# Ranks of the gate's tiles: one behind each of three second-layer matmul groups, in PSUM columns of their own

## The chip, the cores and the metric

The kernel runs on one core of one Trainium2 chip. The metric is the device time of one execution in microseconds, as the median of the runs shown. One more execution was recorded by the hardware profiler; its rows are what the text reads. TensorE is called PE in the rows, VectorE DVE, ScalarE ACT, GpSimd POOL and SyncE SP.

## What is computed

Three layers in a row: an attention, a dense feed-forward layer of 2304 tokens with 2048 hidden units, and a layer of 8 experts of which each token takes the one with the largest gate logit. Cut to what matters:

```python
# attention: a local band (|i - j| < 4) plus attention on means of 4 rows; 4 batches x 8 heads x 576 x 64
x = np.ascontiguousarray(attn_out.transpose(0, 2, 1, 3)).reshape(B * S, H * D)   # 2304 x 512
h = x @ w_in                                                                     # 512 -> 2048
sp = np.where(h > 20.0, h, np.log1p(np.exp(np.minimum(h, 20.0))))
x = (h * np.tanh(sp)) @ w_out                                                    # 2048 -> 512
...
logits = x @ w_gate + modality_bias[modality_id]                                 # 8 experts
e_idx = np.argmax(logits, axis=1)
...
for e in range(E):
    mask = e_idx == e
    h = np.maximum(x[mask] @ w1[e], 0.0)                                         # 512 -> 1024
    out[mask] = gate_w[mask, None] * (h @ w2[e])                                 # 1024 -> 512
```

## The kernel before

The 2304 tokens of the dense layer are cut into five blocks (512, 512, 512, 384 and 384 tokens, numbered 0 to 4), a block into tiles of 128 tokens (four or three). The 2048 hidden units are 16 chunks of 128, worked in steps of four chunks (`GF = 4`), so a block has four steps, `gi` 0 to 3. A step of `moe1` does two loops over its four chunks. In the first, `layer1` makes a chunk's hidden values in one of the PSUM banks bk0 to bk3 (line 698, 12 matmuls per chunk) and `act1` begins the activation. In the second, `mish` ends the activation (ScalarE's sine, then VectorE's line 718, which reads the bank) and `finish` splits the product in two parts (line 727), while `layer2` runs one step behind: it multiplies a chunk of the step before with the second weights and adds to the banks from bk4 on, one bank for each tile. One call of `layer2` is called a second-layer group here: line 738, three matmuls of 512 columns for each tile, so 12 in a block of 512 tokens and 9 in one of 384.

When a block is done, its tiles are gated while the next block runs. `gates` hands out, a few at a time, the 8 dots of each tile (line 621, VectorE, 512 wide); behind the eighth, `gate_l` finds the tile's experts (lines 632 to 642) and the tile goes to the list `done`. Last comes the rank, `gate_r`: each token's place among the tokens of its expert, over all tiles so far. PE multiplies the tile's one-hot rows with a triangle (line 652) and adds the running count `run` of all tiles before (line 653), in 8 columns of a PSUM bank (columns 16 to 23 of bk0; of bk7 in the last block). VectorE reads them (line 656), makes the place (lines 657 to 659) and adds the tile to `run` (line 660). POOL scatters the token numbers to that place in DRAM (line 661), and SP stores the tile's logits (line 651). Ranks have to be made in the order of the tiles, since each one needs the count that the one before left.

The order on every engine is the order in which the code is written; nothing reorders it. In the second loop of a step all tiles in `done` are ranked behind the second group (`n == 1`). With the pace of `gates`, the first tile of a block is done in step 1, two tiles in step 2, and the fourth, where there is one, in step 3. So in step 2 of each of the blocks 1 to 4 two ranks stand directly behind each other. These are called a pair below, and the blocks are named after the block that runs at that time. The last three tiles of all are ranked later, in the expert layer (`rest`). In block 4, `ahead_2` also stands in this loop: it splits the weight pieces of the first experts, VectorE converting one (line 963) and POOL subtracting (line 964). `fixed_slot` (its count is line 664) then picks the experts to begin with.

Of the kernel before, what the change touches and what calls it, by code (L numbers as in the profile page):

```python
# [15 lines left out]
ALU = mybir.AluOpType  # L16
# [7 lines left out]
def moe_kernel(ctx: ExitStack, tc: tile.TileContext, q, k, v, w_in, w_out, modality, w_gate, w_gate_t, m_bias, w1, w2, out):  # L24
    nc = tc.nc
    V, A, G, PE, SP = nc.vector, nc.scalar, nc.gpsimd, nc.tensor, nc.sync
# [4 lines left out]
    E = w_gate.shape[1]  # L31
# [27 lines left out]
    def table(name, shape, dt=F32):  # L59
        return cp.tile(shape, dt, name=name)  # L60
# [6 lines left out]
    ebase = table("ebase", [128, E])  # L67
# [6 lines left out]
    tri = table("tri", [128, 128], BF16)  # L74
    one_b = table("one_b", [128, 128], BF16)
# [6 lines left out]
    bk = [psp.tile([128, 512], F32, name=f"bk{i}") for i in range(8)]  # L82
    gps = bk[7]
# [141 lines left out]
    def prep_step(n=1):  # L225
        for _ in range(n):
            if "wo" in wpool or steps[0] < 4 * (2 * GF + 4):
                next(pg, None)
                steps[0] += 1

    def prep_to(n):
        while ticks[0] < min(n, len(order) + LAG):
            next(pg)
            steps[0] += 1
# [369 lines left out]
    rank = cp.tile([128, E], F32, name="rank")  # L604
    run = cp.tile([128, E], BF16, name="run")
# [10 lines left out]
    def gate_v(tl, es):  # L616

        if 0 in es:
            gate[tl] = cp.tile([128, E], F32, tag="g_ll", name="g_ll")
        for e in es:  # L620
            V.scalar_tensor_tensor(wgb["junk"], x2[tl], 1.0, wgb[e], op0=ALU.mult, op1=ALU.mult, accum_out=gate[tl][:, e:e + 1])  # L621
# [7 lines left out]
    def gate_l(tl):  # L629
        lg = cp.tile([128, E], F32, tag="g_lg", name="g_lg", bufs=3)  # L630
        SP.dma_start(out=x2d[128 * tl:128 * tl + 128, :DM], in_=x2.pop(tl))
        V.tensor_tensor(lg, gate.pop(tl), bias[:, tl], op=ALU.add)
        mx = cp.tile([128, 8], F32, tag="g_mx", name="g_mx")
        ix = cp.tile([128, 8], U32, tag="g_ix", name="g_ix")
        ixf = cp.tile([128, 1], F32, tag="g_if", name="g_if")
        oh = cp.tile([128, E], F32, tag="g_oh", name="g_oh", bufs=3)
        ohb = cp.tile([128, E], BF16, tag="g_ob", name="g_ob", bufs=3)
        V.max(mx, lg)
        V.max_index(ix, mx, lg)
        V.tensor_copy(ixf, ix[:, 0:1])  # L640
        V.tensor_scalar(oh, iota_e, ixf, None, op0=ALU.is_equal)
        V.tensor_copy(ohb, oh)
        gate[tl] = (lg, oh, ohb)
# [2 lines left out]
        gate_p(tl)  # L646
        gate_l(tl)

    def gate_r(tl, gps=gps):
        lg, oh, ohb = gate.pop(tl)  # L650
        SP.dma_start(out=x2d[128 * tl:128 * tl + 128, DM:], in_=lg)
        PE.matmul(gps[:, 16:16 + E], tri, ohb, start=True, stop=False)
        PE.matmul(gps[:, 16:16 + E], one_b, run, start=False, stop=True)
        pf = cp.tile([128, 1], F32, tag="g_pf", name="g_pf")
        pi = cp.tile([128, 1], I32, tag="g_pi", name="g_pi", bufs=2)
        V.tensor_tensor(rank, gps[:, 16:16 + E], ebase, op=ALU.add)
        V.tensor_tensor(rank, rank, oh, op=ALU.mult)
        V.tensor_reduce(pf, rank, axis=X, op=ALU.add)
        V.tensor_copy(pi, pf)
        V.tensor_tensor(run, run, ohb, op=ALU.add)  # L660
        G.indirect_dma_start(out=ids_d, out_offset=bass.IndirectOffsetOnAxis(ap=pi, axis=0), in_=tok_id[:, tl:tl + 1], in_offset=None, bounds_check=E * NT - 1, oob_is_err=True)  # L661
# [8 lines left out]
    def tiles(j):  # L670
        return range(T0[j] // 128, (T0[j] + BLK[j]) // 128)

    def load_x(j, kk, t):

        xf[j, kk] = t[:, :BLK[j]]
        SP.dma_start(out=xf[j, kk], in_=xT[128 * kk:128 * kk + 128, T0[j]:T0[j] + BLK[j]])
# [12 lines left out]
    def layer1(j, f):  # L689
        if j == 0:  # L690
            prep_chunk(f)
        wh, wl = wi[f // QF]
        h = bk[f % GF][:, :BLK[j]]
        n = 0
        for kk in range(KD):
            x = pool["x"][:, :, kk, :BLK[j]]
            for a, c in ((wh, 0), (wh, 1), (wl, 0)):
                PE.matmul(h, a[:, f % QF, kk], x[:, c], start=n == 0, stop=n == 3 * KD - 1)  # L698
                n += 1

    def act1(j, f):
        t = pool["t"].tile([128, BT], F32, tag="t", name="t")[:, :BLK[j]]
        if f % GF == 0:
            d = pool["t"].tile([1, 1], F32, tag="d", name="d", bufs=2)
            A.activation(d, half[:1], AF.Sigmoid)
        A.activation(t, bk[f % GF][:, :BLK[j]], AF.Tanh, scale=0.5)  # L706
        A.activation(t, t, AF.Arctan, scale=-0.5, bias=half)  # L707
        th[j, f] = t

    def mish(j, f):  # L710
        t = th.pop((j, f))
        A.activation(t, t, AF.Sin, scale=-2.0, bias=hpi)  # L712
        if late:
            j_, f_, t_, _ = late[-1]
            gg = gt[j_, f_] = pool["b"].tile([128, 2, BT], F32R, tag="gg", name="gg", bufs=GB)[:, :, :BLK[j_]]
            A.copy(gg[:, 0], t_)  # L716
            late[-1] = (j_, f_, t_, gg)
        V.tensor_tensor(t, bk[f % GF][:, :BLK[j]], t, op=ALU.mult)  # L718
        late.append((j, f, t, None))

    def finish():

        j, f, t, gg = late.pop(0)
        if gg is None:
            gg = gt[j, f] = pool["b"].tile([128, 2, BT], F32R, tag="gg", name="gg", bufs=GB)[:, :, :BLK[j]]
            A.copy(gg[:, 0], t)  # L726
        V.tensor_tensor(gg[:, 1], t, gg[:, 0], op=ALU.subtract)  # L727
# [21 lines left out]
    def moe1(bcx, wop):  # L749
        pool["b"] = bcx.enter_context(tc.tile_pool(name="b_wk", bufs=4))  # L750
        for n in range(GF):
            mish(0, n)
            if n:
                finish()

        todo, done = [], []
        for s in range(GF, NB * NF, GF):
            j, f = divmod(s, NF)
            gi = f // GF
            last = gi == NF // GF - 1  # L760
            more = j + 1 < NB
            dec = s <= NF

            def gates(n):
                for _ in range(n):
                    if todo:
                        tl, e = todo.pop(0)
                        gate_v(tl, [e])
                        if e == E - 1:
                            gate_l(tl)  # L770
                            done.append(tl)

            if gi == 1 and j:
                todo += [(tl, e) for tl in tiles(j - 1) for e in range(E)]
            for n in range(GF):
                layer1(j, f + n)
                prep_step(TK1[2 * n])
                if n == 0 and late:
                    finish()
                act1(j, f + n)  # L780
                prep_step(TK1[2 * n + 1])
                if s == NF and n == 2:
                    prep_to(len(order) + LAG)
                    constants_a()
                if not more:
                    ahead_1(gi, n)
                if gi:
                    gates(3)
            if last and j == 0:
                xs = [stp.tile([128, 2, BT], F32, tag="st", name="xs") for _ in range(2)]  # L790
                for kk in range(KD):
                    load_x(1, kk, xs[kk // 2][:, kk % 2])
            for n in range(GF):
                mish(j, f + n)
                prep_step(TK2[2 * n])
                if n:
                    finish()
                layer2(s - GF + n)
                if last and more:
                    split_x(j + 1, n)  # L800
                prep_step(TK2[2 * n + 1])
                if s == NF and n == 2:
                    constants_b(bk[0])
                if n == 1:
                    while done:
                        gate_r(done.pop(0), bk[0] if more else gps)
                if gi:
                    gates(2 if n == 0 else 1)
                if j and more and (gi, n) in ((1, 3), (2, 3)):
                    for kk in range(2 * gi - 2, 2 * gi):  # L810
                        load_x(j + 1, kk, mtp.tile([128, BT], F32, tag="m", name="xs"))
                if not more:
                    ahead_2(gi, n)
        finish()
        for n in range(GF):
            layer2(NB * NF - GF + n)
            ahead_2(NF // GF, n)
# [382 lines left out]
```

## Time and profile before

| | |
|---|---|
| median of 3 runs | 857.98 us (856.6 to 859.43) |
| the profiled execution | 856.72 us, its span 855.0 us |
| PE busy | 777.9 us (91%) |
| VectorE busy | 608.5 us (71%) |
| ScalarE busy | 538.7 us (63%) |
| POOL busy | 224.5 us (26%) |
| mean granted clock of TensorE | 0.955 of full speed |

The span goes from the first to the last instruction of the profiled execution. Busy shares are means over stages that differ: the attention, the dense layer (about 200 to 590 us) and the experts behind it. PE is the engine that the dense layer waits for most of the time, so its list of waits is the view to begin with.

### The profile page before, as it was taken

The numbers are of one execution on the slowest core, as the hardware profiler recorded it, in microseconds if no ns is written. First come the engines' busy times: TensorE is split into PE (matmuls) and PEld (weight loads), VectorE is DVE, ScalarE is ACT, GpSimd is POOL, SyncE is SP. The second block draws the span as 40 slices with busy tenths as digits, with TensorE's granted clock in tenths as the row PEclk, the third lists the DMA queues.
The fourth block names the chain that finished last, engine by engine and source line by source line (L and its number), as shares of the span: only waits on it lengthen the run. The fifth ranks groups of instructions, "written<-read, shape, count | busy, mean of one in ns | idle before, by whom it ended". The sixth has DMA issues, their size and how long they took to land. (4 is left out here: it accounts for less than half of the span.)

```text
span 855.0 us, 14553 instructions
## 1 busy us (share of the span) xinstructions
PE 777.9 (91%) x5110; PEld 654.9 (77%) x5110; DVE 608.5 (71%) x1442; ACT 538.7 (63%) x1003; POOL 224.5 (26%) x212
## 2 busy tenths in 40 slices
PE   6799986799979999999999799979888999999992
PEld 5577664578858878887889689878787889999982
DVE  6799998789975874288248846979776666656652
ACT  4889997798856556655655566644435555555651
POOL 7678764000000000000000001236533123333330
PEclk9789999889989999999999999989989999999997
DMA  8988983546514110011001105425737777777662
GB/s 175 219 197 227 209 213 124 178 143 192 175 49 165 51 38 0 13 45 33 0 1 56 33 0 210 68 12 167 163 124 231 225 247 225 236 225 222 205 204 83
DMA packets 90641, 115.08 MB, mean 135 GB/s; under 512 B 39467, under 2 KB 61629, under 8 KB 90301
## 3 DMA queue, kind: packets, MB, share of 16 engines
q1 hardware_dynamic: 85997, 103.45, 43.9%
q0 software_dynamic: 4560, 10.60, 3.6%
q8 instruction: 42, 0.69, 0.4%
q14 instruction: 42, 0.34, 0.2%
HBM read 98.11 MB, written 16.17 MB: 134 GB/s over the span
## 5 line engine op out<-in xcount | busy, mean ns | idle before, releaser
L718 DVE TENSOR_TENSOR t<-bk,t 128x512 f32<-128x512 f32 (+1 forms) x80 | 50.2, 633 | 94.1 <-ACT t L712 94.1
L661 POOL DMA_INDIRECT ids_by_expert<-tok_id,g_pi x18 | 19.7, 1096 | 288.0 <-DVE run L660 113.2
L621 DVE SCALAR_TENSOR_TENSOR junk<-o,wgb 128x512 f32<-128x512 f32 x120 | 85.0, 708 | 3.0
L706 ACT ACTIVATE t<-bk 128x512 f32<-128x512 f32 (+1 forms) x80 | 44.1, 551 | 59.3 <-PE bk L698 57.4
L727 DVE TENSOR_TENSOR gg<-t,gg 128x512 fp32r<-128x512 f32 (+1 forms) x80 | 54.8, 685 | 14.1 <-ACT gg L726 7.6
L716 ACT CAST gg<-t 128x512 fp32r<-128x512 f32 (+1 forms) x60 | 34.5, 575 | 47.1 <-DVE t L718 28.8
L698 PE MATMUL bk<-x,wi0h 128*128 128x512 f32 (+1 forms) x160 | 51.1, 398 | 6.3 <-DVE x L686 5.1
L707 ACT ACTIVATE t<-t,half 128x512 f32<-128x512 f32 (+1 forms) x80 | 54.6, 682 | 2.6
L1086 POOL DMA_INDIRECT out_dram<-yo,oid x19 | 25.4, 1336 | 111.4 <-ACT yo L1085 65.1
L698 PE MATMUL bk<-x,wi1h 128*128 128x512 f32 (+1 forms) x160 | 48.2, 384 | 5.9 <-DVE t L718 5.9
L712 ACT ACTIVATE t<-t,hpi 128x512 f32<-128x512 f32 (+1 forms) x80 | 52.3, 674 | 0.2
L1072 ACT ACTIVATE hT<-bk 128x256 fp32r<-128x256 f32 x80 | 30.3, 383 | 33.5 <-PE bk L1070 30.6
L738 PE MATMUL bk<-wo1h,gg 128*128 128x512 f32 x144 | 49.5, 417 | 0.0
L1073 DVE SCALAR_TENSOR_TENSOR hT<-bk,hT 128x256 fp32r<-128x256 f32 x80 | 32.9, 420 | 23.2 <-ACT hT L1072 23.2
L698 PE MATMUL bk<-x,wi3h 128*128 128x512 f32 (+1 forms) x160 | 46.2, 370 | 0.0
L698 PE MATMUL bk<-x,wi2h 128*128 128x512 f32 (+1 forms) x160 | 46.1, 369 | 0.0
L738 PE MATMUL bk<-wo3h,gg 128*128 128x512 f32 x144 | 46.1, 392 | 0.0
L738 PE MATMUL bk<-wo0h,gg 128*128 128x512 f32 x144 | 45.9, 392 | 0.0
L738 PE MATMUL bk<-wo2h,gg 128*128 128x512 f32 x144 | 45.8, 392 | 0.0
L698 PEld LDWEIGHTS bk<-x,wi0h 128*128 128x128 f32 x160 | 31.3, 199 | 14.5 <-DVE x L686 7.0
L698 PEld LDWEIGHTS bk<-x,wi1h 128*128 128x128 f32 x160 | 30.9, 196 | 10.8 <-DVE t L718 6.4
L386 ACT COPY spare<-bk 64x512 f32<-64x512 f32 x32 | 35.3, 1104 | 5.7 <-PE bk L375 5.5
(309 smaller groups left out, 2393.1 us busy)
## 6 DMA issues: line engine op xcount, KB each, us to landing
est<-in_moe_w_dram SPq DMA_DIRECT2D x88, 512.0 KB
wst<-in_moe_w_in_dram SPq DMA_DIRECT2D x16, 512.0 KB
wst<-in_moe_w_out_dram SPq DMA_DIRECT2D x16, 512.0 KB
vw<-in_v_dram SPq DMA_DIRECT2D x88, 64.0 KB
v<-in_v_dram SPq DMA_DIRECT2D x16, 288.0 KB
x_t<-x SPq DMA_DIRECT2D x16, 288.0 KB
x_second<-o SPq DMA_DIRECT2D x18, 256.0 KB
kn<-in_k_dram SPq DMA_DIRECT2D x8, 512.0 KB
```

The costliest lines, as they stand in the source:

```text
L386: A.copy(kb[r, h, 4:4 + n].rearrange("d (p r) -> d r p", r=CT), pk[r].rearrange("d (r p) -> d r p", r=CT))
L621: V.scalar_tensor_tensor(wgb["junk"], x2[tl], 1.0, wgb[e], op0=ALU.mult, op1=ALU.mult, accum_out=gate[tl][:, e:e + 1])
L698: PE.matmul(h, a[:, f % QF, kk], x[:, c], start=n == 0, stop=n == 3 * KD - 1)
L706: A.activation(t, bk[f % GF][:, :BLK[j]], AF.Tanh, scale=0.5)
L707: A.activation(t, t, AF.Arctan, scale=-0.5, bias=half)
L712: A.activation(t, t, AF.Sin, scale=-2.0, bias=hpi)
L716: A.copy(gg[:, 0], t_)
L718: V.tensor_tensor(t, bk[f % GF][:, :BLK[j]], t, op=ALU.mult)
L727: V.tensor_tensor(gg[:, 1], t, gg[:, 0], op=ALU.subtract)
L738: PE.matmul(acc[t], gg[:, a, c], w[:, f % QF], start=f == 0 and n == 0, stop=f == NF - 1 and n == 2)
L1072: A.activation(hT[:, 0, f], ps[:, :256], AF.Relu)
L1073: V.scalar_tensor_tensor(hT[:, 1, f], ps[:, :256], 0.0, hT[:, 0, f], op0=ALU.max, op1=ALU.subtract)
```

## The change

`ready` is taken from `done` once, before the second loop of a step. Behind each of the groups `n` = 1, 2 and 3 one tile of it is ranked, in the columns from `8 * n`. So the first of a pair stays behind group 1 (columns 8 to 15) and the second goes behind group 2 (columns 16 to 23). With one tile ready nothing moves but its columns.

```diff
-    def gate_r(tl, gps=gps):
+    def gate_r(tl, gps=gps, c0=16):
         lg, oh, ohb = gate.pop(tl)
         SP.dma_start(out=x2d[128 * tl:128 * tl + 128, DM:], in_=lg)
-        PE.matmul(gps[:, 16:16 + E], tri, ohb, start=True, stop=False)
-        PE.matmul(gps[:, 16:16 + E], one_b, run, start=False, stop=True)
+        PE.matmul(gps[:, c0:c0 + E], tri, ohb, start=True, stop=False)
+        PE.matmul(gps[:, c0:c0 + E], one_b, run, start=False, stop=True)
...
-        V.tensor_tensor(rank, gps[:, 16:16 + E], ebase, op=ALU.add)
+        V.tensor_tensor(rank, gps[:, c0:c0 + E], ebase, op=ALU.add)
...
-        todo, done = [], []
+        todo, done, ready = [], [], []
...
+            ready, done = ready + done, []
             for n in range(GF):
                 mish(j, f + n)
...
-                if n == 1:
-                    while done:
-                        gate_r(done.pop(0), bk[0] if more else gps)
+                if n and ready:
+                    gate_r(ready.pop(0), bk[0] if more else gps, 8 * n)
```

PE in step 2 of block 1, before: the two ranks between the second and the third second-layer group. A name before the arrow is what is written, behind it what is read; `tri` and `one_b` are the constant factors, `g_ob` a tile's one-hot rows, and a name in brackets is a semaphore that is waited for.

```order
L738 MATMUL bk7_97<-wo1h_2751,gg_3454 128x512
L652 LDWEIGHTS tri_80
L652 MATMUL bk0_90<-g_ob_3478,tri_80 128x8 [waits DVE_49]
L653 LDWEIGHTS one_b_81
L653 MATMUL bk0_90<-run_103,one_b_81 128x8
L652 LDWEIGHTS tri_80
L652 MATMUL bk0_90<-g_ob_3571,tri_80 128x8 [waits DVE_49]
L653 LDWEIGHTS one_b_81
L653 MATMUL bk0_90<-run_103,one_b_81 128x8 [waits DVE_49]
L738 MATMUL bk4_94<-wo1h_2751,gg_3485 128x512 [waits Activation_49]
```

PE in the same step now, around the place of the second rank, behind the third group.

```order
L738 MATMUL bk7_97<-wo1h_2751,gg_3485 128x512
L738 MATMUL bk7_97<-wo1l_2752,gg_3485 128x512
L738 MATMUL bk7_97<-wo1h_2751,gg_3485 128x512
L652 LDWEIGHTS tri_80
L652 MATMUL bk0_90<-g_ob_3571,tri_80 128x8 [waits DVE_49]
L653 LDWEIGHTS one_b_81
L653 MATMUL bk0_90<-run_103,one_b_81 128x8 [waits DVE_49]
L738 MATMUL bk4_94<-wo1h_2751,gg_3519 128x512 [waits Activation_49]
```

The second rank (one-hot rows `g_ob_3571`) went behind the group that reads `gg_3485`; it still waits for VectorE (`DVE_49`) twice.

VectorE in the same step, before: both ranks, then the last dot and the choice of experts of the fourth tile.

```order
L656 TENSOR_TENSOR rank_102<-bk0_90,ebase_73 128x8
L657 TENSOR_TENSOR rank_102<-rank_102,g_oh_3477 128x8
L658 TENSOR_REDUCE g_pf_3634<-rank_102 128x1
L659 CAST g_pi_3635<-g_pf_3634 128x1
L660 TENSOR_TENSOR run_103<-run_103,g_ob_3478 128x8
L656 TENSOR_TENSOR rank_102<-bk0_90,ebase_73 128x8
L657 TENSOR_TENSOR rank_102<-rank_102,g_oh_3570 128x8
L658 TENSOR_REDUCE g_pf_3647<-rank_102 128x1
L659 CAST g_pi_3648<-g_pf_3647 128x1
L660 TENSOR_TENSOR run_103<-run_103,g_ob_3571 128x8
L621 SCALAR_TENSOR_TENSOR junk_3211,g_ll_3577<-o_3312,wgb_3209 128x512
```

VectorE there now, from the end of the first rank to the first instruction of the second.

```order
L660 TENSOR_TENSOR run_103<-run_103,g_ob_3478 128x8
L621 SCALAR_TENSOR_TENSOR junk_3211,g_ll_3577<-o_3312,wgb_3209 128x512
L632 TENSOR_TENSOR g_lg_3645<-g_ll_3577,bias_86 128x8
L638 MAX g_mx_3648<-g_lg_3645 128x8
L639 MAX_INDEX g_ix_3649<-g_mx_3648,g_lg_3645 128x8
L640 CAST g_if_3650<-g_ix_3649 128x1
L641 TENSOR_SCALAR g_oh_3651<-iota_e_72,g_if_3650 128x8
L642 CAST g_ob_3652<-g_oh_3651 128x8
L718 TENSOR_TENSOR t_3560<-bk2_92,t_3560 128x512
L727 TENSOR_TENSOR gg_3659<-t_3542,gg_3659 128x512
L656 TENSOR_TENSOR rank_102<-bk0_90,ebase_73 128x8
```

The second rank's read of bk0 went behind the dot, the choice of experts and the lines 718 and 727 of the third chunk.

POOL in step 2 of block 4, before: the scatters of the pair, then the subtractions of the weight pieces (`est` is a piece as it was loaded, `ew01h` its converted part).

```order
L964 TENSOR_TENSOR ew00l_5504<-est_5304,ew00h_5503 128x1024 [waits DMAHW1_49,DVE_49]
L661 DMA ids_by_expert<-tok_id_74,g_pi_5669 18432x1 [waits DMASW0_49,DVE_49]
L661 DMA ids_by_expert<-tok_id_74,g_pi_5682 18432x1 [waits DMASW1_49,DVE_49]
L964 TENSOR_TENSOR ew01l_5692<-est_5306,ew01h_5691 128x1024 [waits DMAHW2_49,DVE_49,PE_49]
L964 TENSOR_TENSOR ew01l_5692<-est_5302,ew01h_5691 128x1024 [waits DMAHW5_49,DVE_49]
```

POOL there now.

```order
L964 TENSOR_TENSOR ew00l_5504<-est_5304,ew00h_5503 128x1024 [waits DMAHW1_49,DVE_49]
L661 DMA ids_by_expert<-tok_id_74,g_pi_5669 18432x1 [waits DMASW0_49,DVE_49]
L964 TENSOR_TENSOR ew01l_5679<-est_5306,ew01h_5678 128x1024 [waits DMAHW2_49,DVE_49,PE_49]
L661 DMA ids_by_expert<-tok_id_74,g_pi_5701 18432x1 [waits DMASW1_49,DVE_49]
L964 TENSOR_TENSOR ew01l_5679<-est_5302,ew01h_5678 128x1024 [waits DMAHW5_49,DVE_49]
```

One subtraction went ahead of the second scatter. On SP's queue, the load that follows that piece's split went ahead of the second tile's small store in the same way.

## Rows read from the trace of the kernel before

**Rows 1.** PE's waits: what waited for what, us in total, times, longest

```profile
PE bk L652 <- DVE rank L656: 9.9, 4, 5.2
...
PE bk L664 <- DVE run L660: 3.3, 1, 3.3
...
PE bk L653 <- DVE run L660: 2.0, 4, 0.5
```

**Rows 2.** PE's timeline, single ranks (start us, us, engine, line, operation, tiles, shape, count)

```profile
287.89 0.17 PE L653 MATMUL bk<-run,one_b 128*128 128x8 bf16 x1
...
293.46 0.63 PE L698 MATMUL bk<-x,wi2h 128*128 128x512 f32 x2
...
503.13 0.17 PE L653 MATMUL bk<-run,one_b 128*128 128x8 bf16 x1
...
507.34 0.52 PE L698 MATMUL bk<-x,wi0h 128*128 128x384 f32 x2
```

**Rows 3.** PE's timeline, block 1: first rank's line 653, next first-layer matmul

```profile
309.99 0.17 PE L653 MATMUL bk<-run,one_b 128*128 128x8 bf16 x1
...
317.67 0.63 PE L698 MATMUL bk<-x,wi3h 128*128 128x512 f32 x2
```

**Rows 4.** PE's timeline, block 2: the same two

```profile
400.33 0.17 PE L653 MATMUL bk<-run,one_b 128*128 128x8 bf16 x1
...
409.65 0.63 PE L698 MATMUL bk<-x,wi3h 128*128 128x512 f32 x2
```

**Rows 5.** PE's timeline, block 3: both ranks' line 653 (in brackets: idle before, releaser)

```profile
482.10 0.17 PE L653 MATMUL bk<-run,one_b 128*128 128x8 bf16 x1
...
485.08 0.17 PE L653 MATMUL bk<-run,one_b 128*128 128x8 bf16 x1 [0.49 <-DVE run L660]
...
490.68 0.52 PE L698 MATMUL bk<-x,wi3h 128*128 128x384 f32 x2
```

**Rows 6.** PE's timeline, block 4: the same three

```profile
554.19 0.17 PE L653 MATMUL bk<-run,one_b 128*128 128x8 bf16 x1
...
560.21 0.17 PE L653 MATMUL bk<-run,one_b 128*128 128x8 bf16 x1 [0.49 <-DVE run L660]
...
565.77 0.52 PE L698 MATMUL bk<-x,wi3h 128*128 128x384 f32 x2
```

**Rows 7.** Windows around two pairs: busy us by engine, PEclk the granted clock

```profile
309.00:316.00 7.00, 5.22 (x26) 4.07 (x26) 6.29 (x27) 2.59 (x5) 0.98 (x1) 1.00 0.02 3
399.00:407.00 8.00, 6.22 (x24) 4.71 (x23) 7.21 (x29) 2.50 (x5) 0.98 (x1) 0.79 0.03 5
```

**Rows 8.** VectorE's timeline behind the first rank, blocks 1 and 3

```profile
311.24 0.16 DVE L656 TENSOR_TENSOR rank<-bk,ebase 128x8 f32<-128x8 f32 x1
...
313.05 0.69 DVE L621 SCALAR_TENSOR_TENSOR junk<-o,wgb 128x512 f32<-128x512 f32 x1
...
316.19 0.69 DVE L718 TENSOR_TENSOR t<-bk,t 128x512 f32<-128x512 f32 x1
...
486.03 0.69 DVE L621 SCALAR_TENSOR_TENSOR junk<-o,wgb 128x512 f32<-128x512 f32 x1
...
488.91 0.55 DVE L718 TENSOR_TENSOR t<-bk,t 128x384 f32<-128x384 f32 x1
```

**Rows 9.** Timelines of VectorE and POOL, block 4

```profile
541.87 2.79 DVE L727 TENSOR_TENSOR gg<-t,gg 128x384 fp32r<-128x384 f32 x1
...
561.15 0.75 DVE L963 CAST ew01h<-est 128x1024 fp32r<-128x1024 f32 x1
...
568.92 0.98 POOL L661 DMA_INDIRECT ids_by_expert<-tok_id,g_pi  x1 [7.54 <-DVE emx L847]
```

**Rows 10.** VectorE's timeline: three of its waits further on

```profile
502.30 0.56 DVE L718 TENSOR_TENSOR t<-bk,t 128x384 f32<-128x384 f32 x1 [10.32 <-ACT t L712]
...
577.53 1.06 DVE L718 TENSOR_TENSOR t<-bk,t 128x384 f32<-128x384 f32 x2 [1.30 <-ACT t L712]
...
619.68 1.92 DVE L964 TENSOR_TENSOR ew13l<-est,ew13h 128x1024 fp32r<-128x1024 f32 x1 [4.47 <-ACT ew13h L963]
```

## The prediction

> **What bounds the kernel now.** I read the list of PE's waits first, since the change is about an order on PE: which waits there come from the ranks? Two do [rows 1]: the matmul of line 652 waited 9.9 us in four cases for VectorE's read of line 656, and the matmul of line 653 waited 2.0 us in four cases for the running count of line 660. The third row of that group, line 664, belongs to the tail and is not touched by the change; a rival uses it. Then I looked at the four places in PE's timeline. Each of the blocks 1 to 4 has one step (its second with gates) in which two tiles are ready, so that two ranks stand directly behind each other. The second one needs two things of the first: its read (the PSUM columns are the same) and its count. A rank without a neighbour shows what there is without these waits: from line 653 to the next first-layer matmul, with 24 second-layer matmuls between, 5.57 us (287.89 to 293.46), and with 18 of them 4.21 us (503.13 to 507.34) [rows 2]. Behind a pair, counted from the first rank's line 653, it is 7.68 us in block 1 [rows 3], 9.32 us in block 2 [rows 4], 8.58 us in block 3 [rows 5] and 11.58 us in block 4 [rows 6]. PE works without a break on both sides of these places and the other engines are paced by it there, so what is saved there is time of PE's own chain.
>
> Blocks 1 and 2 have the same wait but differ by 1.64 us. The windows say why [rows 7]: around the pair of block 1 the granted clock was 1.00, around that of block 2 it was 0.79, so TensorE ran at 1.2 GHz instead of 2.4 for part of it, after the pause of the pair.
>
> **What the change does, part by part.** No instruction is added or taken away on PE, VectorE or ScalarE. The pieces that move are: the second rank of each pair (on PE two weight loads and two small matmuls) goes behind the next second-layer group; its five VectorE instructions go behind one 512-wide gate dot, a small gate chain and the next group's lines 718 and 727; its two DMAs (a 4 KB store on SP's queue and the scatter on POOL's) go with it. The columns (8 or 16) are new, but PE's second rank still carries a wait for VectorE, and I count nothing for them: by the time the moved rank comes, the first one's read is over in blocks 1 and 2, and in blocks 3 and 4 the count ends later than the read.
>
> What a second rank costs on PE where it does not wait: 24 against 18 matmuls is 1.36 us [rows 2], 0.227 us each, so 24 alone are 5.44 us and a rank's tail adds 0.13 us; with its first matmul (0.03 us) 0.16 us.
>
> Block 1: line 653 of the first rank stands at 309.99. Then two groups and one rank without a wait, 5.57 + 0.16, end at 315.72; the first-layer matmul stood at 317.67. Gain **1.95 us**, if the two things it now needs are there. The count: VectorE begins the first rank at 311.24 and is through both, with a wait between them, at 313.05 [rows 8]; one rank is thus 0.9 us at most, its count is ready at 312.15, and PE asks for it near 312.9. The read: the first-layer matmul writes bank bk0, from which VectorE reads the rank, so it must come after the second read. VectorE reaches that behind 3.14 us of other work (313.05 to 316.19): 312.15 + 3.14 + 0.2 = 315.5, 0.2 us before PE wants the bank. Nothing is paid, but the margin is small.
>
> Block 2: the same times 90.34 us later, so 400.33 + 5.73 = 406.06, where the first-layer matmul stood at 409.65: **3.59 us**, of which 1.64 is the clock. PE has no pause left here, and the rank without a neighbour and block 1's whole stretch ran at 2.4 GHz, so I take the clock as returned; if it is not, 1.95.
>
> Block 3 (three tiles to a group, 18 matmuls): VectorE is late here, and half of the wait stays. 482.10 + 0.03 + 9 matmuls and a tail end at 484.27; the count comes when it came before, at 485.08 [rows 5]. The second group then ends at 487.25, and bank bk0 is free after VectorE's 2.88 us of other work (486.03 to 488.91) [rows 8]: 485.08 + 2.88 + 0.2 = 488.17 at the latest. The first-layer matmul stood at 490.68: **2.51 us**. In the trace the stretch after the pair took 490.68 − 485.08 = 5.60 us instead of 4.21, 1.39 us at the lower clock. If all of that falls on the one group left, it ends at 488.64 and the gain is 2.04. I take 2.51, because less than half of the pause is left.
>
> Block 4: VectorE reaches the first rank 5 us late. PE does one group in that time, then waits for the count until 560.21 as before, and has 9 matmuls behind it instead of 18. They end at 562.38, or at 563.73 if the 1.35 us of lower clock (565.77 − 560.21 − 4.21) stay; the first-layer matmul stood at 565.77 [rows 6]: 3.39 or **2.04 us**. I take 2.04, since a pause of 3.7 us stays, longer than the one after which block 2 lost its clock.
>
> POOL's queue moves in block 4 too. Before, the second scatter stood in front of the subtractions of two weight pieces; it started at 568.92, after 7.54 us in which POOL was idle [rows 9], because one scatter also waits for a DMA ahead of it. Now one subtraction stands in front of that scatter and runs some 7 us earlier, right behind VectorE's conversion of the piece, into VectorE's second rank. A VectorE subtraction that stood beside such POOL work took 2.79 us [rows 9], where a 384-wide one takes 0.55 [rows 8]. The Trainium skill, page "SBUF — State Buffer", section "Who interferes with whom", says that a VectorE instruction with two SBUF inputs and a GpSimd instruction that reads SBUF block each other for the whole instruction; by that rule the second rank's line 657 would stand until POOL is done, and the trace's 2.79 us agrees. From the rows: behind 560.2 come the conversion (0.75 us) [rows 9], two instructions of 0.55, the rank's 0.9 and the 2.24 us of one such hold, which puts the second count at 565.2 at the latest. PE wants it for line 664 behind the next first-layer group (12 matmuls of 384 columns, an estimated 2.05 us at 0.227 for 512), near 564.4 to 565.8. So the price is 0 to 0.8 us; I take 0 and keep 0.8 for the range. SP's next load of a weight piece now stands ahead of the small store and is issued earlier, with room.
>
> Sum: 1.95 + 3.59 + 2.51 + 2.04 = **10.1 us**. The profiled execution took 856.72 us (span 855.0), so 846.6 for it; the median of the three runs, 857.98, lies 1.26 higher, and I carry the sum to it: **847.9 us**.
>
> Is it given back later? In the last step of block 3 VectorE stands 10.32 us waiting for ScalarE [rows 10], whose input is PE's first-layer result, and the other blocks have the same code there: a shift of PE shifts them all. In block 4 VectorE waits for ScalarE in this way at 577.53 [rows 10]. The tail's weight loads start behind that, so they move too.
>
> **The rivals.**
> Forecast with other sizes: no clock returned in block 2 (1.95), the lower clock in block 3 (2.04), 0.8 lost in block 4 (1.24), with block 1's 1.95: 7.2 us, 850.8. With all clock returned in block 4 (3.39): 11.4 us, 846.5.
>
> Block 4 gives its part back: the earlier subtraction on POOL holds VectorE so often that PE waits at line 664. Against it: the margin of a whole first-layer group. Then 8.05 us stay: 849.9. By the rule of the Trainium skill named above it is this place that pays.
>
> Swallowed in the tail: around 619.68 VectorE waits 4.47 us for a converted weight piece [rows 10], and behind it PE waits 3.3 us for line 660 [rows 1]. If those loads do not come earlier when PE does, this wait grows by 10.1 us and the time is 858.0. Against it: the loads are issued as their buffers come free, and these are freed by splits in the last step of block 4, behind that wait at 577.53.
>
> Slower: the read of bank bk0. Behind the change the next first-layer group, with everything after it, hangs on a read that VectorE reaches 3.14 us later than before. This decides from the point where VectorE is more than 0.2 us late in block 1, and it makes that block slower than before once it is 2.15 us late (0.2 + 1.95). Two instructions held as at 541.87 would be 4.48 us: then bank bk0 is free at 319.98 in block 1 (2.31 us after 317.67), at 410.32 in block 2 (0.67 late) and at 492.65 in block 3 (1.97 late), with block 4's 2.04 gained 2.9 us net: 860.9. Against it: POOL does no arithmetic in blocks 1 to 3.
>
> **How the numbers follow.** Forecast 0.71, given back in block 4 0.12, swallowed 0.11, slower 0.05, and 0.01 for better. A measurement of this kernel can tell about 0.3% (2.6 us) from no change. Faster by more than that: the first two, the last and a little of a partly swallowed gain, 0.85; same 0.10; slower 0.05. The range: 846.5 at its best less the 1.4 us by which runs lie under the median gives 845.2; upwards 850.8 and the second case with as much spread, 852.3. That leaves out the swallowed and the slower case.
>
> **What would show it.** Right: in PE's waits the moved ranks (lines 652 and 653 on lines 656 and 660) cost nothing in blocks 1 and 2, about 0.8 us in block 3 and 3.8 us in block 4, some 4.6 us in all where it was 11.9; from the first rank's line 653 to the first-layer matmul 5.7 us in blocks 1 and 2, about 6 in block 3, 8 to 9.5 in block 4; granted clock 1.00 around block 2's pair. Wrong: a new wait of a first-layer matmul for line 656 of more than 1 us in blocks 1 or 2, line 664 waiting in block 4, or a wait near the tail's 664 that grew by what was won.

## The result, and the profile after

| | before | after |
|---|---|---|
| median | 858.4 us of 4 runs (856.6 to 859.43) | 846.87 us of 4 runs (845.84 to 850.68) |
| ratio, 95% interval | | 0.987 (0.9843 to 0.9897) |
| the profiled execution, its span | 856.72 us, 855.0 us | 846.72 us, 845.0 us |
| PE busy | 777.9 us (91%) | 771.7 us (91%) |
| VectorE, ScalarE, POOL busy | 608.5, 538.7, 224.5 us | 605.8, 537.7, 225.9 us |
| mean granted clock | 0.955 | 0.959 |

The changed kernel is faster by 1.3%, 11.5 us by the medians. In its list of PE's waits (what waited for what, us in total, times, longest) these rows answer to [rows 1]:

```profile
PE bk L664 <- DVE run L660: 3.9, 1, 3.9
PE bk L652 <- DVE rank L656: 3.0, 1, 3.0
...
PE bk L653 <- DVE run L660: 0.5, 1, 0.5
```

Lines 652 and 653 waited 11.9 us for the ranks before, now 3.5 us, all of it in block 4. Where the gain lies is in PE's timeline of the changed kernel, the four places of [rows 3 to 6]:

```profile
308.29 0.17 PE L653 MATMUL bk<-run,one_b 128*128 128x8 bf16 x1
...
314.02 0.63 PE L698 MATMUL bk<-x,wi3h 128*128 128x512 f32 x2
...
396.69 0.17 PE L653 MATMUL bk<-run,one_b 128*128 128x8 bf16 x1
...
402.42 0.63 PE L698 MATMUL bk<-x,wi3h 128*128 128x512 f32 x2
...
474.86 0.17 PE L653 MATMUL bk<-run,one_b 128*128 128x8 bf16 x1
477.98 0.23 PE L652 MATMUL bk<-g_ob,tri 128*128 128x8 bf16 x1
...
480.82 0.58 PE L698 MATMUL bk<-x,wi3h 128*128 128x384 f32 x2
...
544.39 0.17 PE L653 MATMUL bk<-run,one_b 128*128 128x8 bf16 x1
...
549.75 0.17 PE L652 MATMUL bk<-g_ob,tri 128*128 128x8 bf16 x1 [3.03 <-DVE rank L656]
550.41 0.17 PE L653 MATMUL bk<-run,one_b 128*128 128x8 bf16 x1 [0.49 <-DVE run L660]
...
553.92 0.74 PE L698 MATMUL bk<-x,wi3h 128*128 128x384 f32 x2
...
556.24 0.18 PE L664 MATMUL bk<-run,one_b 128*128 128x8 bf16 x1
```

From the first rank's line 653 to the next first-layer matmul it is now 5.73, 5.73, 5.96 and 9.53 us in the blocks 1 to 4, where it was 7.68, 9.32, 8.58 and 11.58: gains of 1.95, 3.59, 2.62 and 2.05, in sum 10.21 us. The windows around them (busy us of PE, weight load, VectorE, ScalarE, POOL; then granted clock, DMA share, GB/s; a clock of 1.00 is 2.4 GHz, 0.50 is 1.2 GHz), the first two as in [rows 7], the third around the place that block 2's pair has now:

```profile
309.00:316.00 7.00, 7.00 (x34) 5.59 (x33) 6.44 (x26) 2.96 (x5) 1.24 (x1) 1.00 0.02 3
399.00:407.00 8.00, 8.00 (x38) 6.39 (x37) 5.19 (x19) 3.99 (x6) 1.20 (x1) 1.00 0.02 3
396.00:404.00 8.00, 8.00 (x39) 6.28 (x38) 7.41 (x30) 3.35 (x7) 1.25 (x1) 1.00 0.03 5
474.00:486.00 12.00, 11.17 (x52) 9.55 (x52) 8.43 (x33) 6.28 (x12) 2.06 (x2) 0.86 0.02 2
550.00:556.00 6.00, 5.59 (x21) 4.84 (x21) 5.86 (x13) 1.02 (x3) 3.65 (x2) 0.72 0.67 6
```

In blocks 1 and 2 PE is busy in all of each window. In block 2 the clock is now 1.00, where it was 0.79. In blocks 3 and 4 a part still ran at 1.2 GHz. Block 4 on VectorE and POOL, the changed kernel's timeline:

```profile
551.34 3.33 DVE L727 TENSOR_TENSOR gg<-t,gg 128x384 fp32r<-128x384 f32 x1
...
555.25 0.15 DVE L660 TENSOR_TENSOR run<-run,g_ob 128x8 bf16<-128x8 bf16 x1
...
551.87 2.37 POOL L964 TENSOR_TENSOR ew01l<-est,ew01h 128x1024 fp32r<-128x1024 f32 x1
```

POOL's subtraction now runs between the two ranks, and VectorE's line 727 beside it takes 3.33 us. The second count is there at 555.40, and PE asks for it with line 664 at 556.24 without a wait. Is the gain kept? The first matmul of the expert layer began at 591.51 before, and line 664 in the tail waited 3.26 us there; after:

```profile
579.89 0.28 PE L1070 MATMUL bk<-x,ew00h 128*128 128x256 f32 x1
...
610.82 0.17 PE L664 MATMUL bk<-run,one_b 128*128 128x8 bf16 x1 [3.85 <-DVE run L660]
```

That is 11.62 us earlier, 11.56 at the tail's line 664, and 10.0 at the end. 1.70 us of this was there before the first changed place (block 1's first rank began at 308.29 instead of 309.99), so the part with the change won 9.92 us, and the code behind it took 1.62 us longer. Both of these differences are within what the same code differs by from one execution to the next, as the experiments show.

### The profile page after: what moved, and what is told of

The parts are those of the page before. It is cut to its first block, busy times and chain, and to the rows that moved or that the text cites. A ratio compares the mean times of both kernels' runs of the same rounds, so it can differ in the third digit from the quotient of the medians.

```text
span 845.0 us, 14555 instructions
## 1 busy us (share of the span) xinstructions
PE 771.7 (91%) x5110; PEld 648.8 (77%) x5110; DVE 605.8 (72%) x1442; ACT 537.7 (64%) x1003; POOL 225.9 (27%) x212
## 5 line engine op out<-in xcount | busy, mean ns | idle before, releaser
L727 DVE TENSOR_TENSOR gg<-t,gg 128x512 fp32r<-128x512 f32 (+1 forms) x80 | 57.4, 717 | 7.6 <-ACT gg L716 4.2
```

## The experiments

The runs measure two things: medians against the kernel before on the same chip, and the trace of one execution of each. The ratio that stands with a median, and its interval, are not the quotient of the two medians and lie up to 1.3 us from it. What the trace says is gathered here, worked out from starts of rows as above: line 653 of the first rank to line 698 in each block, and the whole stretch from block 1's first rank to the first matmul of the expert layer (in the kernel before 591.51 − 309.99 = 281.52).

| kernel | block 1 | block 2 | block 3 | block 4 | stretch | against before |
|---|---|---|---|---|---|---|
| before | 7.68 | 9.32 | 8.58 | 11.58 | 281.52 | |
| cols_only | 7.68 | 9.27 | 8.83 | 11.76 | 281.90 | +0.4 |
| order_only | 5.74 | 5.74 | 5.96 | 9.51 | 271.63 | −9.9 |
| after | 5.73 | 5.73 | 5.96 | 9.53 | 271.60 | −9.9 |
| after_again | 5.74 | 5.74 | 5.94 | 9.13 | 271.66 | −9.9 |
| blocks12 | 5.73 | 5.73 | 9.78 | 12.24 | 277.83 | −3.7 |
| block2 | 7.67 | 5.73 | 8.81 | 11.91 | 278.47 | −3.1 |
| blocks34 | 7.69 | 9.29 | 5.94 | 10.04 | 278.02 | −3.5 |
| pool_order | 5.73 | 5.73 | 5.97 | 9.55 | 271.63 | −9.9 |
| group3 | 6.54 | 6.53 | 6.88 | 6.06 | 277.49 | −4.0 |
| group3_bk7 | 5.73 | 5.73 | 5.04 | 6.07 | 270.24 | −11.3 |
| bk7_b3 | 5.73 | 5.73 | 5.04 | 9.40 | 268.56 | −13.0 |
| group3_bk7_late | 5.73 | 5.73 | 5.03 | 6.06 | 266.67 | −14.9 |
| late_again | 5.73 | 5.73 | 5.04 | 6.07 | 266.63 | −14.9 |

What lies around that stretch is the same code in all of them, and its length differs from execution to execution: in these 14 block 1's first rank began between 308.29 and 312.80 us, and the rest behind the stretch took 262.15 to 266.82 us, in no order that follows the edits. Within the stretch the two kernels that were traced twice agree to 0.06 us, and cols_only, with the order of before, lies 0.4 us from it. So the trace tells a cause to some tenths where the granted clock is the same, and a median of a few runs to some 2 us. Where the clock differs, the same code differs by more: block 3 in the order of before took from 8.58 to 9.78 us. The diffs are against the changed kernel.

**Columns or order?**

```diff
 # cols_only: two sets of columns, both ranks behind group 1
-                if n and ready:
-                    gate_r(ready.pop(0), bk[0] if more else gps, 8 * n)
+                if n == 1:
+                    for c0 in (8, 16)[:len(ready)]:
+                        gate_r(ready.pop(0), bk[0] if more else gps, c0)
```

> The columns alone: a pair's two ranks get columns 8 and 16, but both stay behind the second group, as before. Theory (the gain is the place in PE's order): no change, 858 within 2.6 us, and PE's matmul of line 652 still waits about 10 us in four cases for VectorE's line 656. Rival (the shared columns made the wait): those 9.9 us become 2.0 us of waiting for the count, and the time falls by some 8 us to 850. From the profiles of this run and of the kernel before: behind a pair, blocks 1 and 2 take 7.7 us (2.4 GHz) or 9.3 us (partly 1.2 GHz), whichever the clock does in that execution.

```diff
 # order_only: the new order, columns 16 to 23 for every rank
-                    gate_r(ready.pop(0), bk[0] if more else gps, 8 * n)
+                    gate_r(ready.pop(0), bk[0] if more else gps)
```

> The place alone: the second rank behind the third group as in the changed kernel, but in columns 16 to 23 like every other rank. Theory: the whole gain, 847 within 2 us, from the first rank's line 653 to the first-layer matmul 5.7 us in blocks 1 and 2, 6.0 in block 3, 9.5 in block 4. Rival (columns matter): PE waits again for line 656 at the moved rank, 851 or more.

cols_only: 857.21 us against 857.3, ratio 1.0005 (0.9976 to 1.0033). order_only: 844.35 us, 0.9862 (0.9802 to 0.9923), faster than the 845 to 849 us expected; its stretch won 9.9 us, as much as the changed kernel's. The order is the whole change. The waits say why the columns are nothing; of cols_only and of order_only:

```profile
PE bk L652 <- DVE rank L656: 10.0, 4, 5.2
```

```profile
PE bk L652 <- DVE rank L656: 3.0, 1, 3.0
```

With columns of its own the second rank still waits for VectorE's read of the first one, 10.0 us in four cases as in [rows 1], and in the changed kernel 3.03 us in block 4: the program waits by bank. The Trainium skill, page "PSUM — Partial Sum Buffer", section "PSUM bank collisions raise a hardware error", gives this as its rule: guard PSUM by bank and quadrant, not by address, since accesses of two engines collide on disjoint columns too. The program here agrees; a collision was not tried.

**Do the parts add up?**

```diff
 # blocks12: new order in blocks 1 and 2 alone (blocks34, block2: j in (3, 4), j == 2)
                     gate_r(ready.pop(0), bk[0] if more else gps, 8 * n)
+                    while ready and not (j in (1, 2)):
+                        gate_r(ready.pop(0), bk[0] if more else gps, 8 * n)
```

> The change in blocks 1 and 2 alone; in blocks 3 and 4 the pair stays behind the second group. Theory: the four places add up. Blocks 1 and 2 give 1.95 + 3.59 = 5.5 us where the clock falls in one of them before, 3.9 where it falls in none, 7.2 in both: 852.9, between 851 and 854.5. Rival (one wait is exchanged for a later one): blocks 3 and 4 wait longer for it and little is left, 857.

> The change in blocks 3 and 4 alone. Theory: 2.6 + 2.05 = 4.7 us, 853.7; together with the run on blocks 1 and 2 the gains make about 10 us. Rival (VectorE is the bound in these blocks and takes back what PE wins, in the tail or at line 664): 857.

blocks12: 852.89 us, 0.9943 (0.9912 to 0.9975), 4.4 us by the medians. blocks34: 854.73 us, 0.9961 (0.9937 to 0.9984), 2.6 us by the medians. The changed blocks do what they do in the full change, save that block 4 is 10.04 instead of 9.53, with the same waits but a granted clock of 0.53 in the 6 us from 557.3, where it is 0.72 in the changed kernel's window. But the stretches won 3.7 and 3.5, 7.2 us together, where both won 9.9. So the parts don't add up. Of the 2.7 us that are missing, 1.9 went in blocks12 into blocks 3 and 4, whose code is that of before: 9.78 instead of 8.58, and 12.24 instead of 11.58. Is a drop of the clock that is avoided in block 2 only put off to block 3? That was the next run.

> Only block 2 has the second rank behind the next group; blocks 1, 3 and 4 are as in the kernel before. Theory (a drop of the clock belongs to the pause of its own block, and block 2's goes with its pause): from the first rank's line 653 to line 698 7.7 us in block 1, 5.73 in block 2, 8.6 in block 3, 11.6 in block 4; the stretch from block 1's first rank to line 664 in block 4 is 3.6 us shorter than before (257.9). Rival (the drop is only put off to the next pause, as the look at the kernel with blocks 1 and 2 changed suggests): granted clock lower for longer around block 3, 9.8 us there and some 12.2 in block 4, and the stretch is 1.8 us shorter.

855.88 us against 860.2, 0.9937 (0.9913 to 0.9961), 4.3 us by the medians. The stretch won 3.1: block 2's 3.59 less 0.23 in block 3 and 0.33 in block 4, nearer to the theory than to the rival. Windows of 11 us around block 3's pair, blocks12 first, then block2:

```profile
477.00:488.00 11.00, 7.79 (x26) 6.25 (x26) 7.78 (x32) 3.01 (x6) 0.98 (x1) 0.69 0.02 3
```

```profile
480.00:491.00 11.00, 7.49 (x30) 6.17 (x30) 8.64 (x33) 3.65 (x7) 0.98 (x1) 0.84 0.02 3
```

The same instructions with the same waits (1.88 us ahead of the first rank, then 2.16 and 0.49) got a granted clock of 0.69 in one and 0.84 in the other. So block 2's gain is its own: without the pause the clock does not fall there in any of the ten traces with the order of the change, nor in group3's. What a pause costs in clock where one stays is not fixed: block 3's old order took 8.58, 8.81, 8.83 and 9.78 us in four traces. What decides between them these runs don't tell.

**Does the hold by POOL cost anything?**

```diff
 # pool_order: in block 4 POOL's subtraction behind the second scatter
...
         hi_copy(hi, s)
+        if later is not None:
+            put_off.append(lambda: (lo_eng.tensor_tensor(lo, s, hi, op=ALU.subtract), later()))
+            return
...
                     gate_r(ready.pop(0), bk[0] if more else gps, 8 * n)
+                while put_off:
+                    put_off.pop(0)()
...
+            if g == 2 and n == 1:
+                w_split(0, pc, V.tensor_copy, G, lambda: w_load(0, pc + 3, fs["e"]))
+                return
```

> The changed kernel, but in block 4 POOL does its subtraction of the weight piece (and the load behind it is issued) only behind the second scatter, as in the kernel before. Theory (POOL's subtraction holds VectorE's line 727, and block 4 has a margin that covers this): line 727 takes 0.55 us instead of 3.33, the second count (line 660) is ready some 2.8 us earlier, near 552.5, but line 664 on PE did not wait for it, so the time is that of the changed kernel within 0 to 1 us more, because VectorE's chain behind the counts is held by the subtraction instead. Rival (the 3.33 us hold is on the path): 2 to 3 us under the changed kernel. Rival (the earlier subtraction and load are part of the gain, by way of the tail): 2 us or more over the changed kernel.

847.72 us, 0.9893 (0.9856 to 0.993). Timeline of pool_order, VectorE, POOL and PE:

```profile
551.40 0.55 DVE L727 TENSOR_TENSOR gg<-t,gg 128x384 fp32r<-128x384 f32 x1
...
552.53 0.15 DVE L660 TENSOR_TENSOR run<-run,g_ob 128x8 bf16<-128x8 bf16 x1
...
560.89 2.41 POOL L969 TENSOR_TENSOR ew01l<-est,ew01h 128x1024 fp32r<-128x1024 f32 x1
...
556.30 0.18 PE L664 MATMUL bk<-run,one_b 128*128 128x8 bf16 x1
```

With POOL's subtraction elsewhere line 727 takes 0.55 us instead of 3.33, and the count is ready 2.72 us earlier. Line 664 stands where it stood, and the stretch is the same to 0.03 us. The hold is real and costs nothing here. The rule of the Trainium skill named in the prediction (page "SBUF — State Buffer", "Who interferes with whom") agrees: line 727 has two SBUF inputs, and beside a POOL instruction that reads SBUF it took six times as long.

**How late may the second rank stand?**

```diff
 # group3: the second rank behind group 3, still in bank bk0
-                if n and ready:
+                if n in (1, 3) and ready:
```

> The second rank stands one group later, directly ahead of the next first-layer matmul (line 698), and keeps bank bk0; its count is asked for as late as possible. Theory (what bounds the placing from above is VectorE's read of the bank, line 656, ahead of that matmul): VectorE reaches the read behind two more instructions of 0.6 us (0.46 us in block 3), so line 698 waits for line 656 about 0.8 us in each of blocks 1 to 3, 6.5 us from the first rank's line 653 to line 698 in blocks 1 and 2 instead of 5.73. In block 4 the second rank uses another bank and no longer stands in PE's way (line 698 some 3.3 us earlier), but its count now comes behind the subtraction that stands beside POOL, near 556.2, and line 664 waits 3 to 4 us for it: nothing won there. Together 2.5 us longer than the changed kernel: 7.5 to 8 us under the kernel before. Rival (the read does not bind, the bank is free in time): no wait of line 698 for line 656, as fast as the changed kernel, 10 to 13 us under the kernel before.

855.99 us against 857.27, 0.997 (0.9937 to 1.0002): the runs do not tell it apart from the kernel before. The stretch still won 4.0 us; more than half of the gain is gone. Timeline of group3, VectorE's and PE's rows:

```profile
319.13 0.16 DVE L656 TENSOR_TENSOR rank<-bk,ebase 128x8 f32<-128x8 f32 x1
...
319.34 0.51 PE L698 MATMUL bk<-x,wi3h 128*128 128x512 f32 x1 [0.76 <-DVE rank L656]
...
565.08 0.17 PE L664 MATMUL bk<-run,one_b 128*128 128x8 bf16 x1 [3.62 <-DVE run L660]
```

Line 698 waited 0.76 us for the read of the bank in blocks 1 and 2, as expected, and 2.45 us in block 3, where 0.8 was expected; each of the three took 0.8 to 0.9 us longer than in the changed kernel. Block 4 gave its gain back at line 664. Yet the trace lost 5.9 us against the changed kernel, not the 2.5 expected. Two windows of group3 hold the other 3:

```profile
487.00:491.00 4.00, 2.94 (x9) 2.94 (x10) 2.02 (x8) 2.13 (x4) 0.00 (x0) 0.59 0.00 0
565.00:570.00 5.00, 4.92 (x20) 4.92 (x20) 3.78 (x23) 3.03 (x6) 0.70 (x1) 0.66 0.35 27
```

Behind line 698's wait in block 3 (2.45 us) and line 664's (3.62 us) TensorE ran at 1.2 GHz for a part of each window. From block 3's line 698 to block 4's first rank it is 65.01 us instead of 63.57, and from line 664 to the expert layer 25.21 instead of 23.65: 1.44 and 1.56 us longer, so that each wait was paid once more in clock.

**Another bank, and a later use of the counts**

```diff
 # group3_bk7: in blocks 3 and 4 bank bk7, second rank behind group 3 (bk7_b3: j == 3 for the place)
-                if n and ready:
-                    gate_r(ready.pop(0), bk[0] if more else gps, 8 * n)
+                if n in ((1, 3) if j > 2 else (1, 2)) and ready:
+                    gate_r(ready.pop(0), gps if j > 2 else bk[0], 8 * n)
 # group3_bk7_late, late_again: the same, and the step with line 664 one group later
-        if g == NF // GF - 1:
-            if n == 0:
+        if g == NF // GF - 1 and n:
+            if n == 1:
                 fs[1] = fixed_slot(1)
```

> Blocks 1 and 2 as changed; in blocks 3 and 4 the second rank stands behind the last of the four groups and both ranks use the other bank, bk7. Theory (in blocks 3 and 4 PE waits because VectorE is late, and what PE has to do meanwhile sets how much of that is paid): in block 3 the 1.9 us wait of the first rank for line 718 goes with the bank, and the second rank needs no wait: 4.2 us from the first rank to line 698 if the clock stays at 1.00, some 2.9 us earlier than in the changed kernel. In block 4 line 698 comes 3.3 us earlier and line 664 waits 3 to 4 us for the count. Together 2.5 to 3 us under the changed kernel, 12.5 to 13 us under the kernel before. Rival (PE is paced there by VectorE anyhow, and a pause taken away comes back at the next gate): no change against the changed kernel, 10 us under the kernel before.

849.29 us, 0.9897 (0.984 to 0.9954); 1.4 us under the changed kernel in the stretch, not the 2.5 to 3 expected. Block 3 is 2.9 us shorter, as expected: 0.92 in the table's column, since no read holds line 698's bank, and 2.01 ahead of the first rank, where the wait of 1.87 us for line 718 is gone. Bank and place were changed together; their shares are read from the waits and were not tested apart. Block 4's line 698 came 3.5 us sooner; that was paid at line 664, once as a wait of 3.62 us, which was expected, and once as clock (0.72 from 554 to 560), which was not.

> As the kernel with bank bk7 in blocks 3 and 4, and the step that needs the total counts (line 664) starts one group later in block 4. Theory (block 4's gain is a matter of when the count is asked for): line 664 waits for nothing or under 1 us, so the 3.3 us of block 4 are kept, about 5 to 6 us under the changed kernel, 15 to 16 us under the kernel before, less the part that the tail gives back because its weight loads do not come earlier (in the changed kernel it gave back 1.8 us of the shift). Rival (the tail is set by VectorE's chain behind the counts): what block 4 wins is lost in the waits of line 664 and of the chain behind it, 12.5 us under the kernel before, as without the later start.

844.0 us, 0.9837 (0.9811 to 0.9863). Timeline of group3_bk7_late:

```profile
479.03 0.17 PE L653 MATMUL bk<-run,one_b 128*128 128x8 bf16 x1 [0.49 <-DVE run L660]
479.06 0.42 PE L698 MATMUL bk<-x,wi3h 128*128 128x384 f32 x1
...
547.90 0.17 PE L652 MATMUL bk<-g_ob,tri 128*128 128x8 bf16 x1 [1.01 <-DVE rank L656]
...
554.58 0.17 PE L664 MATMUL bk<-run,one_b 128*128 128x8 bf16 x1 [1.58 <-DVE run L660]
```

One group later line 664 waits 1.58 us, and behind it the clock stayed at 1.00 up to 562. The wait did not fall under 1 us as expected, so 1.6 of block 4's 3.5 us are paid there and 1.9 are kept. With block 3's 2.9 the stretch is 4.9 us shorter than the changed kernel's, just short of the 5 to 6 us expected. The three remaining runs set these beside each other on one chip.

> The changed kernel, with bank bk7 and the last group for the second rank in block 3 alone; block 4 as changed. Theory (what the two later placings do adds up): block 3's first rank does not wait for line 718, 2.9 us earlier than in the changed kernel at block 3's line 698 and at line 664; 12 to 13 us under the kernel before. Rival (block 4 gives it back, since VectorE is late there anyhow): line 664 as in the changed kernel, 10 us under the kernel before.

> The changed kernel once more, beside the next one on the same chip: 10 to 11 us under the kernel before; 3.5 us of waits for lines 656 and 660 at the moved ranks.

> The kernel with bank bk7 in blocks 3 and 4, the second rank behind the last group there and the later start of the step with line 664, once more: from the segments of its first look, 2.9 us (block 3) and 1.8 us (block 4) under the changed kernel, so 14 to 16 us under the kernel before. Rival (its first result was the chance of a tail): no more than 12 us under it.

Against 860.2 us of the kernel before: after_again 847.91 us, 0.986 (0.9837 to 0.9883); bk7_b3 846.04 us, 0.9829 (0.9804 to 0.9854); late_again 844.95 us, 0.9827 (0.9801 to 0.9854). late_again's stretch is 14.9 us under the kernel before, as in the first run of this code. after_again is 12.3 us under it by the medians and 9.9 in the stretch, where 10 to 11 were expected, and its moved ranks wait 4.0 us, not 3.5, since block 3 waits 0.49 us for the count at the full clock. The medians put late_again 3 us under after_again, with intervals that still overlap; the traces put this code 4.9 to 5.0 us under the changed kernel in both of its executions. So group3_bk7_late is the best of these kernels, by the traces clearly and by the medians probably. bk7_b3, which leaves block 4 as changed, has 3.1 of these 5 us.

## Why the prediction was right

The forecast, 847.9 us, was 1.0 us above the median. The mechanism held and so did all four terms, two of them with some luck (blocks 3 and 4).

**What bounds.** PE's own chain did: 8.4 us of its waits and the 1.64 us of clock in block 2 went, and the stretch became 9.9 us shorter. One sentence did not hold: PE did not work without a break on both sides of block 3's pair. Ahead of the first rank it stood 1.88 us for VectorE's line 718, which reads bank bk0 too; in the waits of the kernel before, as of the changed one, this is the row

```profile
PE bk L652 <- DVE t L718: 1.9, 1, 1.9
```

The forecast counts from behind this wait and so is not touched by it, but it is 1.9 us that another bank takes away (group3_bk7).

**Blocks 1 and 2.** 1.95 and 3.59 us were forecast and measured; 5.73 us is what the single rank gave [rows 2]. The choice between 3.59 and 1.95 in block 2 was right: without the pause the clock did not fall there in any trace.

**Block 3.** 2.51 forecast, 2.62 measured, though the reason given about the clock was wrong. It was said to be returned there; the window shows 0.86. It made next to no difference. The forecast had VectorE's read of bank bk0 as the step's end (488.17), and PE at the lower clock came to line 698 only 0.10 us after that read was over. In the second trace of the changed kernel, with the full clock there, the read is what holds it. VectorE's read in the changed kernel, then the timeline of after_again:

```profile
480.57 0.15 DVE L656 TENSOR_TENSOR rank<-bk,ebase 128x8 f32<-128x8 f32 x1
```

```profile
482.25 0.16 DVE L656 TENSOR_TENSOR rank<-bk,ebase 128x8 f32<-128x8 f32 x1
...
482.46 0.62 PE L698 MATMUL bk<-x,wi3h 128*128 128x384 f32 x2 [0.61 <-DVE rank L656]
```

At 2.4 GHz PE waits 0.49 us for the count and 0.61 for the bank and needs 5.94 us; with a part at 1.2 GHz it waits for nothing and needs 5.96. For this reason, mostly, the waits came to 3.5 us, not the 4.6 forecast; after_again has 4.0.

**Block 4.** 2.04 forecast with the lower clock kept, 2.05 measured with a clock of 0.72 in its window. That the two agree so closely is luck: in after_again, where the clock fell later, it is 2.45. POOL's hold came as forecast, on line 727 and not 657; the forecast went by line 727 beside this row of the kernel before:

```profile
541.82 2.41 POOL L964 TENSOR_TENSOR ew00l<-est,ew00h 128x1024 fp32r<-128x1024 f32 x1
```

The hold was 2.78 us (3.33 − 0.55) instead of the 2.24 reckoned, and the instructions around it took as much less. The count was ready 11.0 us after the first rank's line 653 (555.40 − 544.39), just the latest time reckoned (565.2 − 554.19); PE asked for it after 11.85, so the price was 0, with 0.84 us to spare.

**The rivals.** Given back in block 4: pool_order shows no price. Swallowed: the tail's line 664 waits 3.85 us instead of 3.26, not 10 more, and comes 11.56 us earlier. Slower by the bank's read: the margin was 0.46 us in block 1 (read over at 313.56, matmul at 314.02) where 0.2 was reckoned, and group3 shows the mechanism is real, 0.76 us a block once two more instructions stand ahead.

**The rest.** Forecast sum 10.1, measured at the places 10.21, in the stretch 9.92 and 9.86, by the medians 11.5 and 12.3. The last two differ from the others by less than unchanged code before and behind the stretch differs from execution to execution, so that the median came within 1.0 us of the forecast is in part chance too.

## What to carry to other kernels

Where two small steps depend on each other through another engine, put work that is ready between them, but no more than that engine needs: here one group (2.7 us in blocks 1 and 2) won 9.9 us, and one more in the same bank left 4.0 of them, because the next user of the same bank or count came too soon. Ask of each moved read who wants its bank next, and by when; another bank and a later use of the result moved the limit here, to 14.9 us. Splitting columns of one bank buys nothing where waits go by bank.

## What was not expected of the hardware

A wait of PE can be paid twice, once as the wait and once as clock behind it, and the second part is not fixed. Behind block 2's pair the old order had the lower clock in each of its three traces and took 9.27 to 9.32 us; behind block 1's, with the same waits (1.29 and 0.49 us), it had 2.4 GHz in each of four traces and took 7.67 to 7.69 us. Line 664's wait of 3.62 us was followed by 1.2 GHz in group3 and group3_bk7 and cost 1.56 us more; the one of 1.58 us in group3_bk7_late and late_again was not. And in block 3 of the changed kernel the lower clock cost 0.02 us (5.96 against 5.94), because PE at the full clock has to wait there for VectorE's read.
